# Sliding-window attention and a gMLP on one Trainium2 core: the same steps in a new hand-written order, with 75 passes on other engines and 37 products in another form

## The chip, the cores and the metric

One core of a Trainium2 chip (trn2). The metric is device time in microseconds of one execution. Each kernel is run several times; the median is given with the lowest and the highest run. A profiled execution gives a trace: every instruction's start and duration, by engine. The engines are TensorE (PE, with its weight loads as PEld), VectorE (DVE), ScalarE (ACT), GpSimd (POOL) and SyncE (SP), which here only issues DMAs.

## The reference

Inputs are float32: q, k, v of shape 8 x 8 x 576 x 64 (batch, heads, positions, head size), and the weights of the gMLP. The output is 8 x 576 x 512.

```
scores = q @ k^T / 8                          # per batch and head
scores = where(0 <= t - s < 64, scores, -1e9) # causal window of 64
attn   = softmax(scores);  x = attn @ v       # heads side by side: x is 8 x 576 x 512
h      = relu(x @ w_in);   u, v2 = h[..., :512], h[..., 512:]
v_n    = (v2 - mean(v2)) / sqrt(var(v2) + 1e-6)         # over the last axis
v_s    = w_spatial @ v_n + b_spatial          # mixes positions, per batch
out    = (u * v_s) @ w_out
```

## The kernel before, in words

**Work.** The eight batches go one after the other through attention (two groups g of four heads) and the gMLP, overlapped. Each batch's 576 positions are four tiles of 128 and a remainder of 64. The remainder's attention is done for both groups together (name ending `_r`), in batches 4 and 5, and 6 and 7, for two batches at once (PAIRS). Compute is in float16 with float32 sums in PSUM.

**Steps.** All work is cut into about 1100 named steps, each on one engine. A step's name has its batch, its group or tile:

- `ldq ldk ldv` are DMA loads issued by SP (lines 412, 433); `ldwin ldwsp ldwo ldb` load the weights and the bias; `st` are stores.
- `cq ck cv`, `cwin cwsp cwo cb` cast what was loaded to float16 (helper `cp`, lines 290 to 300; on GpSimd a q or k tile is three casts of 384 columns, line 295). `tq tk` are VectorE's 32x32 transposes of q and k (line 419). `sl su s4` copy v into a shifted layout (lines 449 to 459).
- `S` are the scores (TensorE, line 479), `E` the exponentials (ScalarE, 486), `M` the mask as a minimum (VectorE, 489), `Z` the row sums by a product with ones (TensorE, 502), `N` and `n` the logarithm and exp(-log) that invert them (ScalarE, 529, 531), `P` the product with v (514), `X` the scaling of it (VectorE, 522). The remainder's scores are on line 553, its `Z_r` on 582, `P_r` on 597.
- `V` and `U` are x @ w_in's two halves (TensorE, 614 or 617; the last tile of V together with the previous batch's last tile of the output, 702 and 705). `Vr` and `Ur` evict them with a ReLU (ScalarE, 669 and 763). `Vb Va` are VectorE's mean and variance (671, 673), `L1 L2` ScalarE's 1/sqrt (716, 718), `A` the normalisation (VectorE, 728).
- `G` is the product with the transposed w_spatial (five contraction tiles kk, the last with the bias row), `Ge` its eviction times u (VectorE, 797), `O` the product with w_out, `Oe` its copy out of PSUM (line 647), then the store.
- `W` transposes w_spatial on TensorE (378), `We` copies it out (384). `D` are warming steps: two matmuls of zeros into a bank that nobody reads (862); two of the 27 have nine short ones instead (line 149).

**Order.** Nothing schedules at run time. `ORDER` (line 18) lists every step with its engine and its buffers: `V0_2:PE:1` is batch 0, tile 2, on TensorE, in PSUM bank 1. Each engine runs its steps in the listed order and waits at semaphores for what the step's instructions read or overwrite. `DQ` is SP's queue of DMA issues. The pairs of numbers behind the steps' names in the code, such as `("ACT", 0.49)`, are the engines that a step may have and its planned cost; they are not used at run time.

**Forms.** `halves` (line 612) emits a gMLP product in one of two forms. With `PE` in the list each matmul has 128 weight columns (line 614). With `PH` each is two matmuls of 64 weight columns, into the lower and the upper half of the PSUM bank (line 617).

**Buffers.** Eight buffers for natural tiles (`nat`), four for v, nine for the transposed ones, four PSUM banks and two pairs of banks (the scores). A load is issued when the buffer's last reader is done.

## Time and profile before

| | us |
|---|---|
| runs: lowest, median, highest | 195.38, 195.44, 198.58 |
| profiled execution: from its first to its last instruction (the span) | 193.6 |
| what the median has beside that span | 1.84 |
| TensorE busy in the span | 184.9 |
| VectorE, ScalarE, GpSimd busy | 163.7, 157.1, 87.4 |
| first scores S0_0 start on TensorE | 9.26 |
| second group of batch 1, S1_1, starts | 29.85 |
| first G product starts | 38.69 |
| last product starts | 188.93 |

The page gives the span of the profiled execution and not its whole time; the runs above were timed without a profile. HBM was read for 32.79 MB and written for 9.44 MB, 218 GB/s over the span.

How to read the rows that follow: a row of a timeline is start, duration, engine, line, operation, out<-in, shape, count, and in brackets the idle time of the engine before it with what ended it. Alike instructions that follow each other are one row, and its duration goes from the first one's start to the last one's end. Matmuls are pipelined, so a row's duration has the last one's way through the array in it; the distance from one product's start to the next one's is what it costs. A row of a view by stage is from:to, length, then busy time and count of each engine. A group's row is line, engine, operation, out<-in, shape, count, busy us, mean ns of one, and idle us before it.

### The profile page before, as it was taken

Reading aid. Unit: us, or ns where it says so; the run is one execution under the profiler, and the core shown is the slowest. Engines: PE = TensorE matmul, PEld = TensorE weight load, DVE = VectorE, ACT = ScalarE, POOL = GpSimd, SP = SyncE. Lnnn points to the kernel's source line nnn. Section 1 sums busy time; section 2 is a strip of 40 time slices with the busy share of each in tenths; the row PEclk is TensorE's granted clock in tenths of the full one; section 3 lists DMA queues with packets and bytes.
Section 4 is the critical chain, followed back from the end, with each engine's and each line's share of the span. In section 5 each row is a group of like instructions: output and inputs, shape, how many; then the busy total and the mean of one; then the engine's idle time right before and its main releaser. Section 6 shows DMA issues by size and latency. Waiting matters only on the chain.

```text
span 193.6 us, 7606 instructions
## 1 busy us (share of the span) xinstructions
PE 184.9 (95%) x3218; PEld 107.0 (55%) x3218; DVE 163.7 (85%) x304; ACT 157.1 (81%) x282; POOL 87.4 (45%) x161
## 2 busy tenths in 40 slices
...
GB/s 177 373 316 290 391 355 333 168 275 373 242 205 332 261 335 179 149 38 289 367 230 184 310 310 282 196 177 218 306 125 266 22 3 0 224 30 0 135 166 191
DMA packets 50421, 42.73 MB, mean 221 GB/s; under 512 B 39377, under 2 KB 39761, under 8 KB 50386
## 3 DMA queue, kind: packets, MB, share of 16 engines
...
q8 instruction: 25, 0.41, 0.9%
...
HBM read 32.79 MB, written 9.44 MB: 218 GB/s over the span
## 4 chain that ended last, share of the span: by engine, by line
PE 70%; DVE 13%; ACT 9%; DMA 3%; issue 2%; SPq 1%
PE bank L617 50%; PE bank L614 4%; PE pair L479 4%; PE bank L514 3%; DMA nk<-in_k_dram 3%; PE bank L502 3%; ACT e L486 3%; DVE qT L419 2%; PE bank L702 2%; DVE e L489 2%; DVE kT L419 2%; DVE st L671 2%; DVE g L797 1%; DVE x L522 1%; ACT lz L529 1%
## 5 line engine op out<-in xcount | busy, mean ns | idle before, releaser
L617 PE MATMUL bank<-wspT,vn 128*64 128x512 f16 (+3 forms) x530 | 39.1, 296 | 0.0
L486 ACT ACTIVATE e<-pair 128x1024 f16<-128x1024 f32 x32 | 32.0, 1030 | 1.6 <-PE pair L479 1.4
L797 DVE TENSOR_TENSOR g<-bank,ru 128x512 f16<-128x512 f32 (+1 forms) x36 | 23.3, 654 | 9.4 <-PE bank L617 7.0
L647 ACT COPY ob<-bank 128x512 f32<-128x512 f32 (+1 forms) x38 | 21.9, 591 | 9.7 <-PE bank L617 8.4
L669 ACT ACTIVATE vs<-bank 128x512 f16<-128x512 f32 (+1 forms) x40 | 23.8, 602 | 7.1 <-PE bank L705 5.6
L617 PE MATMUL bank<-x,win 128*64 128x512 f16 (+2 forms) x304 | 29.1, 327 | 0.0
L617 PEld LDWEIGHTS <-vn 128*64 128x64 f16 (+1 forms) x530 | 20.8, 111 | 13.2 <-issue 0.2
L671 DVE BATCH_NORM_STATS2 st<-vs 128x6 f32<-128x512 f16 (+1 forms) x40 | 26.0, 670 | 2.3 <-ACT vs L669 2.2
L298 POOL COPY hs<-hv 64x512 f16<-64x512 f16 (+1 forms) x36 | 20.1, 585 | 16.3 <-ACT hv L292 8.4
L617 PE MATMUL bank<-win,x 128*64 128x512 f16 x216 | 27.0, 379 | 0.0
L617 PE MATMUL bank<-wout,g 128*64 128x512 f16 (+1 forms) x208 | 24.7, 371 | 0.0
L522 DVE TENSOR_TENSOR x<-bank,lz 128x512 f16<-128x512 f32 x32 | 21.2, 684 | 3.5 <-PE bank L514 2.2
L489 DVE TENSOR_TENSOR e<-e,mask 128x1024 f16<-128x1024 f16 x32 | 23.0, 725 | 0.5 <-ACT e L486 0.4
L763 ACT ACTIVATE ru<-bank 128x512 f32<-128x512 f32 (+1 forms) x38 | 21.6, 584 | 1.5 <-PE bank L617 0.8
L295 POOL CAST hk<-nk 128x384 f16<-128x384 f32 x36 | 19.4, 574 | 7.1 <-DMA nk<-in_k_dram 6.7
L529 ACT ACTIVATE lz<-bank 128x512 f32<-128x512 f32 x32 | 19.0, 599 | 1.9 <-PE bank L502 1.6
L298 POOL CAST hv<-nv 128x512 f16<-128x512 f32 x18 | 11.7, 661 | 18.8 <-DMA nv<-in_v_dram 18.7
L419 DVE STREAM_TRANSPOSE kT<-hk 128x576 f32<-128x576 f32 x16 | 19.9, 1241 | 0.2 <-ACT hk L292 0.2
L419 DVE STREAM_TRANSPOSE qT<-hq 128x576 f32<-128x576 f32 x16 | 19.8, 1237 | 0.2
L531 ACT ACTIVATE lz<-lz 128x512 f32<-128x512 f32 x32 | 19.6, 642 | 0.0
L295 POOL CAST hq<-nq 128x384 f16<-128x384 f32 x27 | 14.9, 588 | 10.3 <-DMA nq<-in_q_dram 7.8
L617 PEld LDWEIGHTS <-win 128*64 128x64 f16 x304 | 14.4, 110 | 9.2
...
## 6 DMA issues: line engine op xcount, KB each, us to landing
...
nv<-in_v_dram SPq DMA_DIRECT2D x64, 128.0 KB, 5.9
...
wi<-in_moe_w_in_dram SPq DMA_DIRECT2D x8, 256.0 KB, 5.8
...
wo<-in_moe_w_out_dram SPq DMA_DIRECT2D x4, 256.0 KB, 7.2
```

The lines of the kernel that those rows point to most:

```text
L295: nc.gpsimd.tensor_copy(o[:, n:n + 384], i[:, n:n + 384])
L298: nc.gpsimd.tensor_copy(o[:, lo:hi, :, :], i[:, lo:hi, :, :])
L419: d = add(f"t{name}{b}_{g}", ("DVE", 1.09), key, lambda e: nc.vector.transpose(qt.t[:, :].rearrange("p (i j) -> p j i", j=18), h.t[:, :].b ...
L486: ex = add(f"E{b}_{g}{u}", ("ACT", 0.91), key, lambda e, u=u: nc.scalar.activation(e2[u].t[:, :, :], sc[u].t[:, :, :], AF.Exp, bias=0.0, s ...
L489: mins.append(add(f"M{b}_{g}{u}", ("DVE", 0.65), key, lambda e, u=u: nc.vector.tensor_tensor(e2[u].t[:, :, :], e2[u].t[:, :, :], mask[:, : ...
L522: lambda e, u=u, ob=ob, lz=lz: nc.vector.tensor_tensor(x.t[:, u, :], ob.t[:, :], lz.t[:, :], ALU.mult),
L617: nc.tensor.matmul(o[c:c + 64, :], w[:, c:c + 64], x, start=start, stop=stop)
L647: lambda e: (nc.vector.tensor_copy if last else nc.scalar.copy)(view(), m.t[rows, 0:n]),
L669: rl = add(f"Vr{b}_{j}", ("ACT", 0.49), key, lambda e: nc.scalar.activation(vs.t[0:jn, :], m.t[0:jn, :], AF.Relu), deps=[pv], acq=[vs], us ...
L671: s1 = add(f"Vb{b}_{j}", ("DVE", 0.6), key + 0.02, lambda e: nc.vector.bn_stats(st6.t[0:jn, 0:6], vs.t[0:jn, :]), deps=[rl], acq=[st6], us ...
L763: lambda e, m=m, ru=ru, n=n: nc.scalar.activation(ru.t[:, 0:n], m.t[:, 0:n], AF.Relu), deps=[pu], acq=[ru], uses=[m])))
L797: nc.vector.tensor_tensor(g.t[:, 0:n], m.t[:, 0:n], ru.t[:, 0:n], ALU.mult)
```

## The change

ORDER is another list of the same steps without seven of the warming steps: 27 become 20, all of two matmuls of 512 columns. Every engine's sequence is new, SP's of the loads and stores too, and the buffers are dealt anew.

75 passes have another engine. From ScalarE to VectorE: seven `Oe`, seven `Ur`, five `Vr`, and `cwin110 s40_0 sl1_11 su1_00`. From ScalarE to GpSimd: 18 casts and copies, among them `ck3_1 cq7_0 cq7_1`, five `cv` and `cwo00`. From VectorE to GpSimd: ten, among them `cq1_1 cq6_0`. From VectorE to ScalarE: `ck0_0 cq0_0 cq0_1 We0 We4 sl0_10 Oe7_3 Oe7_4`. From GpSimd to ScalarE: `cb ck2_0 cv5_10 s46_0`, two `sl` and three `su`; to VectorE: `ck6_0 cwsp0`, three `sl` and two `su`. In sum ScalarE has 24 steps fewer, VectorE and GpSimd 12 more each.

37 gMLP products have the other form: 23 halved ones become full (V0_3, V1_1, V1_2, V2_0, V2_1, U0_2, U0_3, U1_1, U1_3, U1_4, U2_0, G1_4, G7_0 to G7_4, O6_2, O6_3, O7_0, O7_2, O7_3, O7_5) and 14 full ones halved (U1_0, U2_2, U2_4, U3_2, U3_3, U3_4, G2_0, G2_2, G2_3, G2_4, O1_1, O1_2, O1_3, O2_2).

The diff, with ORDER cut to the start (up to the first G products) and the close (from V7_4 on):

```diff
@@ ORDER @@
-D24:PE:0 ldb:DQ:0 D5:PE:1 D21:PE:2 ldk0_0:DQ:1 ck0_0:DVE:0 tk0_0:DVE:0 D18:PE:3 D2:PE:2 D14:PE:2
-D19:PE:3 D10:PE:0 ldq0_0:DQ:2 ldk0_1:DQ:3 ldv0_00:DQ:0 ldq0_1:DQ:4 ldv0_10:DQ:1 D3:PE:3 ldv0_11:DQ
-cv0_10:POOL:0 ldk1_0:DQ:5 ck0_1:ACT:1 ldv0_12:DQ ldv0_13:DQ ldv0_01:DQ cq0_0:DVE:2 ldq1_0:DQ:6
-tq0_0:DVE:1 ldv0_02:DQ D1:PE:2 S0_0:PE:0:1 tk0_1:DVE:2 D22:PE:0 E0_01:ACT:0 E0_00:ACT:1 cq0_1:DVE:3
-tq0_1:DVE:3 D15:PE:3 D6:PE:1 D0:PE:2 D26:PE:0 D23:PE:3 S0_r:PE:1:0 E0_r0:ACT:0 E0_r1:ACT cv0_11:POOL
-sl0_10:DVE:0 M0_00:DVE ldv0_03:DQ su0_10:DVE M0_01:DVE ck1_0:DVE:0 M0_r:DVE D8:PE:1 Z0_00:PE:2
-ldv0_04:DQ ldwin110:DQ:7 ldv0_14:DQ ldwin111:DQ ldwin100:DQ:1 S0_1:PE:1:0 N0_00:ACT:0 E0_11:ACT:2
-D16:PE:0 D7:PE:3 E0_10:ACT:3 M0_11:DVE Z0_01:PE:1 Z0_r:PE:2 D4:PE:0 Z0_11:PE:3 N0_r:ACT:1
-N0_01:ACT:2 cv0_00:ACT:1 N0_11:ACT:3 ldwin101:DQ su0_11:DVE M0_10:DVE D12:PE:0 Z0_10:PE:2 D20:PE:1
-sl0_11:POOL tk1_0:DVE:4 sl0_00:ACT:1 N0_10:ACT:4 n0_11:ACT n0_10:ACT cq1_0:POOL:2 tq1_0:DVE:5
-ldq1_1:DQ:2 ldk1_1:DQ:3 P0_10:PE:0 P0_11:PE:3 cwin110:ACT n0_01:ACT D11:PE:1 cv0_01:POOL
-ldwin000:DQ:4 ldwin010:DQ:5 ldwin001:DQ ldwin011:DQ ldwsp1:DQ:6 X0_10:DVE:0 su0_00:DVE X0_11:DVE
-n0_00:ACT sl0_01:POOL cb:POOL su0_01:POOL S1_0:PE:0:1 D25:PE:2 D13:PE:1 P0_00:PE:0 X0_00:DVE:1
-E1_01:ACT:3 s40_1:ACT P0_01:PE:2 D9:PE:3 cwin111:POOL cwin100:POOL cwin101:POOL ck1_1:POOL:1
-s40_0:ACT E1_00:ACT:2 cwin010:POOL X0_01:DVE cwin001:POOL cwin011:POOL V0_2:PE:1 M1_01:DVE
-Vr0_2:ACT:0 n0_r:ACT P0_r:PE:3 Z1_01:PE:0 V0_0:PE:2 ldwsp3:DQ:0 M1_00:DVE N1_01:ACT:5 Vr0_0:ACT:1
-cq1_1:DVE:3 Z1_00:PE:1 V0_3:PH:0 V0_1:PE:2 N1_00:ACT:4 cwin000:ACT Vr0_3:ACT:2 Vr0_1:ACT:3
-ldwsp0:DQ:7 ldwsp4:DQ:1 ldwsp2:DQ:2 cwsp1:POOL:6 ldv1_00:DQ:2 ldq2_0:DQ:3 X0_r:DVE:0 tq1_1:DVE:7
-Vb0_2:DVE:0 V0_4:PE:3 tk1_1:DVE:8 S1_1:PE:1:0 cwsp3:POOL:0 cwsp0:POOL:1 Vb0_0:DVE:1 Vb0_3:DVE:2
-Vr0_4:ACT:4 Va0_3:DVE Vb0_4:DVE:3 Va0_4:DVE Va0_0:DVE Va0_2:DVE Vb0_1:DVE:4 Va0_1:DVE U0_2:PH:1
-U0_3:PH:0 ldk2_0:DQ:4 U0_4:PE:2 ldv1_01:DQ ldv1_02:DQ ldv1_03:DQ E1_11:ACT:1 E1_10:ACT:0 cwsp2:POOL
-cq2_0:POOL:0 M1_10:DVE ldv1_10:DQ:3 Ur0_2:ACT:0 L10:ACT:0 ldv1_11:DQ ldv1_12:DQ ldv1_13:DQ L20:ACT
-ldv1_14:DQ ldq2_1:DQ:5 ldv1_04:DQ ldk2_1:DQ:6 ldwo00:DQ:0 ldwo01:DQ Ur0_4:ACT:1 S1_r:PE:0:1
-Z1_10:PE:3 U0_0:PE:1 ldwo10:DQ:7 ldwo11:DQ U0_1:PE:2 E1_r0:ACT:0 Ur0_3:ACT:2 E1_r1:ACT Ur0_0:ACT:3
-N1_10:ACT:3 A0_0:DVE:0 A0_3:DVE:1 cwsp4:DVE Ur0_1:ACT:4 W1:PE:0 W3:PE:1 W2:PE:3 W0:PE:2 A0_1:DVE:2
-A0_4:DVE M1_11:DVE We1:DVE M1_r:DVE n1_00:ACT We2:ACT We3:ACT A0_2:DVE:3 We0:DVE W4:PE:0 ldq3_0:DQ:1
-ldk3_0:DQ:2 ldv2_00:DQ:1 ck2_0:POOL:2 We4:DVE D17:PE:3 Z1_11:PE:1 Z1_r:PE:2 G0_0:PH:3 G0_1:PH:0
...
-Ge6_4:DVE:0 Ge6_1:DVE:1 st5_4:DQ st5_1:DQ st5_0:DQ G6_0:PH:3 Ge6_0:DVE:2 Vb7_2:DVE:5 V7_4:PE:0
-U7_1:PH:2 G6_3:PH:3 Vr7_4:ACT:2 Oe6_4:ACT:0 Ur7_1:ACT:5 Ur7_3:ACT:0 Vb7_1:DVE:2 Va7_0:DVE
-Vb7_4:DVE:4 Va7_4:DVE Ge6_3:DVE:3 Va7_1:DVE Va7_2:DVE L17:ACT:1 L27:ACT A7_4:DVE A7_1:DVE:4
-A7_0:DVE:5 A7_2:DVE:6 U7_2:PH:0 O6_1:PH:2 O6_2:PH:1 O6_0:PH:3 Ur7_2:ACT:3 Oe6_0:ACT:0 Oe6_1:ACT
-O6_3:PH:0 Oe6_2:ACT:1 Oe6_3:ACT A7_3:DVE:7 G7_0:PH:3 st6_0:DQ st6_4:DQ st6_1:DQ G7_1:PH:2 G7_2:PH:1
-G7_3:PH:0 Ge7_0:DVE:5 Ge7_1:DVE:6 Ge7_2:DVE:7 G7_4:PH:3 Ge7_3:DVE:8 O7_0:PH:2 Oe7_0:ACT:0 st7_0:DQ
-O7_2:PH:1 Oe7_2:ACT:1 Ge7_4:DVE:9 O7_1:PH:0 st7_2:DQ O7_3:PH:3 O7_4:PE:2 Oe7_1:ACT O7_5:PH:1
-Oe7_3:DVE st7_1:DQ st7_3:DQ Oe7_5:ACT Oe7_4:DVE:0 st7_41:ACT st7_40:DQ st7_5:ACT
+D0:PE:0 D1:PE:1 D2:PE:2 D3:PE:3 D4:PE:0 D5:PE:1 D6:PE:2 D7:PE:3 ldv0_00:DQ:0 ldk0_0:DQ:0 ldq0_0:DQ:1
+ck0_0:ACT:0 ldk0_1:DQ:2 cq0_0:ACT:1 tk0_0:DVE:0 tq0_0:DVE:1 ldq0_1:DQ:3 D8:PE:0 D9:PE:1 D10:PE:2
+D11:PE:3 S0_0:PE:0:1 D12:PE:0 ck0_1:ACT:2 D13:PE:1 cq0_1:ACT:3 ldb:DQ:4 tk0_1:DVE:2 tq0_1:DVE:3
+ldk1_0:DQ:5 ldv0_01:DQ ldq1_0:DQ:6 ldv0_10:DQ:1 E0_00:ACT:0 ldv0_11:DQ E0_01:ACT:1 ldv0_02:DQ
+D14:PE:2 D15:PE:3 D16:PE:0 S0_r:PE:0:1 M0_00:DVE ldv0_14:DQ ldv0_03:DQ ldv0_13:DQ Z0_00:PE:1
+M0_01:DVE ldv0_12:DQ cv0_00:POOL:0 sl0_00:POOL:0 cq1_0:POOL:0 cb:ACT E0_r0:ACT:0 cv0_10:POOL:1
+cv0_01:POOL su0_01:POOL su0_00:POOL E0_r1:ACT ldwin110:DQ:7 ldv0_04:DQ N0_00:ACT:0 ldwin100:DQ:0
+Z0_01:PE:2 S0_1:PE:0:1 ldwin111:DQ cv0_11:POOL ck1_0:DVE:1 M0_r:DVE ldwin101:DQ E0_10:ACT:2
+ldq1_1:DQ:1 ldk1_1:DQ:2 tk1_0:DVE:4 N0_01:ACT:1 ldwin010:DQ:3 ldwin000:DQ:4 cwin111:POOL
+cwin100:POOL cwin101:POOL ldwin011:DQ D17:PE:3 Z0_r:PE:0 ldwin001:DQ ldwsp3:DQ:5 cq1_1:POOL:2
+N0_r:ACT:2 sl0_10:ACT:1 ck1_1:POOL:3 ldwsp0:DQ:6 ldwsp4:DQ:0 cwin010:POOL ldwsp2:DQ:1 M0_10:DVE
+tq1_0:DVE:5 E0_11:ACT:3 cwin001:POOL cwin011:POOL ldwsp1:DQ:2 sl0_01:DVE su0_10:DVE M0_11:DVE
+ldq2_0:DQ:3 cwsp3:POOL:6 D18:PE:3 ldv1_00:DQ:2 cwsp2:POOL n0_00:ACT n0_r:ACT ldv1_01:DQ cwsp1:POOL:7
+su0_11:DVE cwin110:DVE sl0_11:DVE s40_0:DVE ldk2_0:DQ:7 Z0_10:PE:3 D19:PE:1 S1_0:PE:0:1 N0_10:ACT:3
+n0_01:ACT s40_1:ACT P0_00:PE:1 Z0_11:PE:2 N0_11:ACT:4 n0_11:ACT n0_10:ACT cwsp4:POOL X0_00:DVE:0
+P0_10:PE:0 P0_r:PE:3 cq2_0:POOL:1 ldv1_03:DQ X0_r:DVE:0 ldv1_02:DQ cv1_00:POOL:2 P0_01:PE:2
+E1_01:ACT:0 P0_11:PE:1 sl1_00:POOL:2 X0_01:DVE X0_10:DVE:1 ldv1_10:DQ:3 V0_4:PE:3 X0_11:DVE
+cv1_01:POOL E1_00:ACT:2 Vr0_4:ACT:0 M1_01:DVE M1_00:DVE V0_0:PE:2 ldv1_11:DQ su1_01:POOL ldv1_13:DQ
+ldv1_12:DQ tq1_1:DVE:8 ldv1_14:DQ V0_2:PE:0 tk1_1:DVE:0 V0_1:PE:1 Vr0_2:ACT:1 cwin000:ACT
+Vr0_1:ACT:2 Vr0_0:ACT:3 V0_3:PE:3 Vb0_2:DVE:0 Vb0_4:DVE:1 ldv2_00:DQ:1 ldk2_1:DQ:4 Z1_01:PE:0
+cv1_10:POOL:3 Va0_2:DVE sl1_10:POOL:3 cv1_11:POOL N1_01:ACT:5 Vr0_3:ACT:4 S1_1:PE:1:0 E1_11:ACT:1
+Vb0_3:DVE:2 Vb0_1:DVE:3 su1_10:POOL U0_2:PE:1 ldq2_1:DQ:5 M1_11:DVE Va0_3:DVE Vb0_0:DVE:4
+ldwo10:DQ:1 Va0_1:DVE ldv1_04:DQ E1_10:ACT:3 Ur0_2:ACT:0 U0_4:PE:2 U0_0:PE:0 Va0_0:DVE Ur0_0:ACT:1
+ldwo00:DQ:2 Va0_4:DVE S1_r:PE:0:1 Z1_11:PE:3 s41_1:POOL U0_3:PE:1 ldwo11:DQ ck2_1:POOL:0 cwsp0:DVE:1
+ldwo01:DQ ldk3_0:DQ:6 U0_1:PE:0 Ur0_4:DVE:2 W2:PE:2 cq2_1:POOL:2 s41_0:POOL cwo10:POOL E1_r0:ACT:0
+L10:ACT:0 E1_r1:ACT L20:ACT Ur0_3:ACT:3 W1:PE:1 A0_1:DVE:0 cwo11:POOL N1_11:ACT:0 A0_2:DVE:1
+M1_r:DVE M1_10:DVE Ur0_1:ACT:4 W4:PE:3 cwo01:POOL We2:ACT A0_4:DVE ldv2_02:DQ ldv2_01:DQ ldq3_0:DQ:0
+ldv3_00:DQ:0 ldv2_03:DQ W0:PE:0 ldv2_10:DQ:3 ldv3_02:DQ ldv2_14:DQ We1:DVE cwo00:POOL We4:ACT
+W3:PE:2 We0:ACT Z1_00:PE:3 Z1_10:PE:1 We3:ACT N1_10:ACT:2 A0_0:DVE:2 ck2_0:ACT:3 A0_3:DVE:3
+tq2_0:DVE:2 G0_3:PH:0 Z1_r:PE:2 Ge0_3:DVE:0 N1_00:ACT:1 G0_0:PH:1 N1_r:ACT:3 n1_10:ACT tk2_0:DVE:3
...
+Ur7_4:DVE:3 G6_2:PH:3 Ge6_3:DVE:1 G6_4:PH:1 Ge6_2:DVE:0 U7_0:PH:0 Ge6_4:DVE:2 G6_0:PH:2 V7_4:PE:3
+Ge6_0:DVE:3 U7_2:PH:1 Va7_1:DVE Vb7_0:DVE:2 Oe6_4:ACT:0 Vr7_4:DVE:0 O6_0:PH:2 Ur7_2:ACT:4 Va7_0:DVE
+Vb7_4:DVE:3 O6_1:PH:3 Oe6_0:ACT:1 Va7_4:DVE Ur7_0:DVE:5 L17:ACT:1 O6_2:PE:1 L27:ACT Oe6_1:ACT
+A7_1:DVE:4 A7_4:DVE O6_3:PE:2 A7_0:DVE:5 Oe6_2:ACT:0 A7_3:DVE:6 A7_2:DVE:7 G7_1:PE:0 Oe6_3:ACT
+st6_1:DQ G7_0:PE:3 st6_0:DQ st6_4:DQ G7_2:PE:1 Ge7_0:DVE:8 Ge7_1:DVE:6 G7_3:PE:2 Ge7_2:DVE:5
+Ge7_3:DVE:7 O7_0:PE:3 O7_2:PE:0 Oe7_0:ACT:0 st7_0:DQ O7_5:PE:1 Oe7_2:ACT:1 G7_4:PE:2 st7_2:DQ
+Oe7_5:DVE O7_3:PE:3 st7_5:ACT Ge7_4:DVE:9 O7_4:PE:0 Oe7_3:ACT O7_1:PH:1 st7_3:DQ Oe7_4:ACT:0
+st7_40:DQ st7_41:ACT Oe7_1:DVE st7_1:DQ
-NWARM, NFILL, FILL = 27, 2, 9
+NWARM = len([w for w in ORDER.split() if w[0] == "D"])
@@ -298,6 +298,12 @@
             ENG[e].tensor_copy(o, i)
+
+    def relu(e, o, i):
+        if e == "ACT":
+            nc.scalar.activation(o, i, AF.Relu)
+        else:
+            nc.vector.tensor_scalar_max(o, i, 0.0)
@@ -643,8 +649,8 @@
         def view():
-        cpy = add(f"Oe{b}_{j}", ("DVE", 0.4) if last else ("ACT", 0.49), key,
-                  lambda e: (nc.vector.tensor_copy if last else nc.scalar.copy)(view(), m.t[rows, 0:n]),
+        cpy = add(f"Oe{b}_{j}", cost(n, p=False, d1=True), key,
+                  lambda e: cp(e, view(), m.t[rows, 0:n]),
@@ -666,8 +672,8 @@
     def stat_steps(b, j, m, vs, pv, key, VS, ST):
-        rl = add(f"Vr{b}_{j}", ("ACT", 0.49), key, lambda e: nc.scalar.activation(
-            vs.t[0:jn, :], m.t[0:jn, :], AF.Relu), deps=[pv], acq=[vs], uses=[m])
+        rl = add(f"Vr{b}_{j}", [("ACT", 0.49), ("DVE", 0.61)], key, lambda e: relu(
+            e, vs.t[0:jn, :], m.t[0:jn, :]), deps=[pv], acq=[vs], uses=[m])
@@ -759,9 +765,9 @@
-            RU.append((ru, add(f"Ur{tag}", ("ACT", 0.06 + 0.00083 * n), key + 0.2 + 0.03 * i,
-                               lambda e, m=m, ru=ru, n=n: nc.scalar.activation(
-                                   ru.t[:, 0:n], m.t[:, 0:n], AF.Relu), deps=[pu], acq=[ru], uses=[m])))
+            RU.append((ru, add(f"Ur{tag}", cost(n, p=False, d1=True), key + 0.2 + 0.03 * i,
+                               lambda e, m=m, ru=ru, n=n: relu(
+                                   e, ru.t[:, 0:n], m.t[:, 0:n]), deps=[pu], acq=[ru], uses=[m])))
@@ -857,9 +863,8 @@
         def emit_D(e, m=m, i=i):
-            for c in range(2 if i < NWARM - NFILL else FILL):
-                n = 512 if i < NWARM - NFILL else 128
-                nc.tensor.matmul(m.t[:, 0:n], scratch[:, 0:128], scratch[:, 0:n], start=True, stop=True)
+            for c in range(2):
+                nc.tensor.matmul(m.t[:, :], scratch[:, 0:128], scratch[:, :], start=True, stop=True)
         add(f"D{i}", ("PE", 0.43), -2.0, emit_D, acq=[m], mode="f")
```

179 lines of the change are left out of this document (88 added, 91 removed).

## The prediction

> **What bounds the kernel now.** I read the page first (busy shares, then the chain that ended last), then the busy time by stage, then the timelines of TensorE and VectorE up to the first G product, then those of the last 20 us.
>
> ```profile
> span 193.6 us, 7606 instructions
> PE 184.9 (95%) x3218; PEld 107.0 (55%) x3218; DVE 163.7 (85%) x304; ACT 157.1 (81%) x282; POOL 87.4 (45%) x161
> PE 70%; DVE 13%; ACT 9%; DMA 3%; issue 2%; SPq 1%
> ```
>
> TensorE is the engine of the chain (70%). The next view splits its time at S0_0 (first scores, 9.25), S1_1 (29.85), the first G product (38.69) and the last product; the one behind it is the same for the warming matmuls (L862) alone.
>
> ```profile
> 9.25:29.85 20.60, 18.98 (x335) 8.85 (x336) 19.29 (x27) 17.73 (x32) 13.17 (x20) 1.00 1.10 333
> 29.85:38.69 8.84, 8.60 (x147) 5.06 (x149) 8.51 (x22) 8.12 (x17) 6.29 (x9) 1.00 0.92 252
> 38.69:189.40 150.71, 150.33 (x2723) 90.53 (x2719) 129.66 (x241) 128.53 (x232) 65.61 (x121) 1.00 0.69 201
> ```
>
> ```profile
> 9.25:29.85 20.60, 8.61 (x46) 3.00 (x46) 1.00 1.10 333
> ```
>
> The columns are PE, PEld, DVE, ACT and POOL busy, the granted clock, the DMA share and GB/s. From 38.69 on TensorE is idle for 0.38 us of 150.71: nothing but less TensorE work, or an earlier start of this stage, can gain there. Before 29.85, 8.6 of its 18.98 busy us are warming, that is, waiting in disguise, while VectorE is busy for 19.29 of 20.60. So the start is paced by VectorE and its suppliers, the rest by TensorE, and a warming step taken out gains nothing by itself.
>
> **The amount of TensorE work.** The new order holds the same real products. Ahead of the first G product (G0_0 before, G0_3 after) the two orders have the same products done but for two small ones, Z1_r before and Z1_00 in both. So the question is when the first G product starts, what TensorE loses after it, and how the kernel closes.
>
> Change of form, 37 products: a full product is 4 matmuls, a halved one 8.
>
> ```profile
> 76.96 2.75 PE L614 MATMUL bank<-wout,g 128*128 128x512 f16 x12
> 79.55 0.63 PE L614 MATMUL bank<-x,win 128*128 128x64 f16 x16
> 177.04 3.62 PE L617 MATMUL bank<-wout,g 128*64 128x512 f16 x32
> 180.50 5.14 PE L617 MATMUL bank<-wspT,vn 128*64 128x512 f16 x80
> 73.81 0.38 PE L502 MATMUL bank<-e,ones 128*64 128x512 f16 x2
> 74.02 1.03 PE L617 MATMUL bank<-x,win 128*64 128x512 f16 x8
> 81.33 0.39 PE L502 MATMUL bank<-e,ones 128*64 128x512 f16 x2
> 81.65 4.04 PE L614 MATMUL bank<-wspT,vn 128*128 128x512 f16 x35
> ```
>
> Three full products go from 76.96 to 79.55, 0.863 us each; four halved ones from 177.04 to 180.50, 0.865. The form itself costs nothing. A switch between 64-column and 128-column weights does: Z then a halved product is 0.21 (73.81 to 74.02), Z then a full one 0.32 (81.33 to 81.65), so 0.1 a switch. Counted in the two orders, there are 16 such switches from the first G product on in both (28 against 23 from S0_0 on, the five being in the start, where waiting covers them). Term: 0.
>
> **The start.** VectorE's and GpSimd's rows of the stage that decides:
>
> ```profile
> 7.16 0.75 DVE L300 CAST hq<-nq 128x1152 f16<-128x1152 f32 x1
> 25.60 1.06 DVE L300 CAST hq<-nq 128x1152 f16<-128x1152 f32 x1
> 28.56 1.23 DVE L419 STREAM_TRANSPOSE kT<-hk 128x576 f32<-128x576 f32 x1
> 37.53 0.82 DVE L300 COPY wspT<-bank 128x576 f16<-128x576 f16 x2
> 17.10 1.90 POOL L295 CAST hq<-nq 128x384 f16<-128x384 f32 x3 [1.02 <-DVE e L489]
> 25.20 2.28 POOL L295 CAST hk<-nk 128x384 f16<-128x384 f32 x3 [1.79 <-DMA nk<-in_k_dram]
> 27.43 1.72 POOL L300 CAST win<-wi 128x512 f16<-128x512 f32 x3
> 17.70 0.33 SPq L412 DMA_DIRECT2D nq<-in_q_dram  x1
> DMA to landing us min/median/max: 5.4/5.9/6.4
> ```
>
> Before, VectorE itself casts q of batch 1, heads 4 to 7 (25.60, 1.06 us), then transposes it, and starts k's transpose tk1_1 at 28.56, though k was cast by 27.48. After, cq1_1 is GpSimd's, ahead of ck1_1. The same loads stand ahead of q1_1 and k1_1 in both orders, and DMA is full (share 1.10), so I leave their landings: q1_1 at 17.70 + 5.4 = 23.1, k1_1 at 25.2. GpSimd: 23.1 + 1.90 = 25.0, then k from 25.2 in 1.72 (three casts undisturbed, the 27.43 row, an upper neighbour in size) to 2.28 (as now): 26.9 to 27.5, I take 27.2. VectorE sheds ck0_0, cq0_0, cq0_1, cq1_1 (0.75 to 1.06 each) and takes cwin110 and three small copies, so it should be free by then: tk1_1 starts at 27.2, 1.4 us earlier.
>
> The first load is now v, one issue and 128 KB ahead of k, and the first casts are ScalarE's (row below: 1.16 instead of 0.75). Both make S0_0 later, by an estimated 0.3 us, but ScalarE takes all four casts and VectorE is free between transposes, so the masks of heads 0 to 3 come no later than now.
>
> ```profile
> L292 ACT CAST hq<-nq 128x1152 f16<-128x1152 f32 x3 | 3.5, 1156 | 0.0
> 29.85 0.67 PE L479 MATMUL pair<-qT,kT 32*128 32x128 f16 x56 [0.42 <-DVE kT L419]
> 35.48 2.39 PE L378 MATMUL bank<-id,wn 128*128 128x128 f16 x25
> 37.80 0.61 PE L862 MATMUL bank<-scratch 128*128 128x512 f16 x2
> ```
>
> From tk1_1 to the first G, VectorE does the same in both orders but for Vb0_2 (0.6) and Ur0_4 (0.41) added and We0 and We4 (0.82 the pair) gone to ScalarE: 28.56 to 38.35 is 9.79, after 9.9. It ends with A0_0 and A0_3: 27.2 + 9.9 = 37.1. G0_3 needs A0_0 first, a third of a us earlier, and A0_3 only with its fourth matmul pair, so it can start at 36.8. TensorE's own chain from S1_1 (27.2 + 1.23 = 28.5) is the 8.84 of now less the warming step at 37.80 (0.54) and a wait of 0.3 at S1_r: 28.5 + 8.1 = 36.6, in time. The W transposes (35.48 now) come some 1.8 us earlier, and the casts of W_spatial that they need, four of them on GpSimd, are taken as in time. **First G product: 36.8 in place of 38.69, -1.9 us.** Bounds: -2.5 (q1_1 and k1_1 landing 0.6 sooner) to -0.8 (the later first casts carry through, 0.3, and both GpSimd casts run as slowly as the slowest now).
>
> **From the first G to the last batch.** 19 of the 75 moved passes are evictions from ScalarE to VectorE, 17 of 512 columns and 2 of 256. VectorE's 512-column copy out of PSUM has no row; bounds are the 256-column copy and the two-input product, and I take the latter, of the same size.
>
> ```profile
> L647 DVE COPY ob<-bank 128x256 f32<-128x256 f32 x1 | 0.4, 426 | 0.1
> L797 DVE TENSOR_TENSOR g<-bank,ru 128x512 f16<-128x512 f32 x32 | 21.8, 684 | 9.3 <-PE bank L617 7.0 <-ACT ru L763 1.4 <-ACT lz L531 0.4
> 60.00:80.00 20.00, 20.00 (x345) 12.20 (x332) 19.50 (x35) 19.56 (x36) 15.12 (x28) 1.00 0.91 253
> 170.00:180.00 10.00, 10.00 (x122) 5.58 (x118) 7.53 (x18) 3.41 (x8) 0.00 (x0) 1.00 0.02 7
> ```
>
> 17 x 0.684 + 2 x 0.42 = 12.5 us more for VectorE (7.3 to 12.5). All but two stand in batches 4 to 7, beside a TensorE that is full while VectorE, in 170 to 180, is busy for 7.5 of 10 us: hidden. Without that cover, each is 0.68 us between a product and the next one on its bank. 28 passes, copies and casts of loads and weights, go to GpSimd and 16 leave it: net three loads of 1.7 us and nine shorter passes, an estimated 10 us on its 87.4, off the chain. In 60 to 80 VectorE is busy for 19.5 of 20: there a lead of TensorE can be spent by waiting for it. Counted in the order, VectorE's work ahead of S3_1 falls from 60 to 54 us while TensorE's falls from 47 to 44, so most of the lead should hold. I take **+0.3** (bounds -0.4, the idle time of now, and +1.9, all of the lead).
>
> One rule speaks against this. VectorE's cast of 1152 took 0.75 us while GpSimd rested (7.16) and 1.06 while it cast (25.60). The Trainium skill, page "SBUF — State Buffer", section "Who interferes with whom", says that VectorE in a two-port mode, or with two inputs in SBUF, and GpSimd block each other for a whole instruction; the rows agree. By that rule ck1_1 would take its 2.28 again, and the start would gain 1.6 in place of 1.9.
>
> **The close.**
>
> ```profile
> 185.11 0.69 DVE L797 TENSOR_TENSOR g<-bank,ru 128x512 f16<-128x512 f32 x1 [0.39 <-PE bank L617]
> 188.93 0.61 PE L617 MATMUL bank<-wout,g 128*64 128x256 f16 x8
> 189.57 0.37 ACT L835 COPY ob<-bank 128x256 f32<-128x256 f32 x1 [0.72 <-PE bank L617]
> 190.31 0.54 ACTq L838 DMA_DIRECT2D out_dram<-ob  x1
> out_dram<-ob SPq DMA_DIRECT2D x3, 256.0 KB, 2.1
> out_dram<-ob ACTq DMA_DIRECT2D x1, 128.0 KB, 2.4
> ```
>
> G7_3's last matmul is issued by 184.83 (20 pairs of halves at 0.216 from 180.50), Ge7_3 ends at 185.80, 0.97 later. Now G7_4 (0.63) stands between G7_3 and O7_0; after, O7_0 follows at once, and its fourth matmul, 0.65 in, waits 0.3. G7_4 comes later, with one half-size product (0.44, the 188.93 row to 189.37) ahead of O7_4, which waits about 0.2 for Ge7_4 (256 wide, 0.4). **+0.5**. After the last product, now 189.37 by issue: copy to 189.94, store issued at 190.31 behind another, landing 2.4 later, 192.7. After, the last is the full O7_1: copied by VectorE (0.2 + 0.68), issued at once on SP, 2.1 to land: 3.05 against 3.35. **-0.25**, rounded.
>
> **Sum.** -1.9 + 0.3 + 0.5 - 0.25 = -1.35. Against the profiled execution: span 193.6 - 1.35 = 192.25. The median of the runs is 195.44, 1.84 above that span; what lies around it is taken as unchanged: 194.1 us.
>
> **Rivals.**
> - *The lead is spent* (20%): GpSimd's extra 10 us slow VectorE's masks and casts (1.06 against 0.75) while VectorE is already at 19.5 of 20, and TensorE waits for 1.9 us more between 40 and 130. Against it: VectorE has less listed ahead of each S. Time: 195.44 + 0.5 - 0.25 = 195.7.
> - *TensorE runs cold* (10%), the case on the slower side. At the start it needs 6.87 us for 20 matmuls:
>
> ```profile
> 1.27 6.87 PE L862 MATMUL bank<-scratch 128*128 128x512 f16 x20 [1.27 <-DVE scratch L237]
> ```
>
>   At the 0.216 of the rows of 76.96 (12 in 2.59), 20 would take 4.3, so a cold stretch costs 2.5 us. After S0_0 the order keeps 8 warming steps of 17, and only D18 and D19 between the masks of heads 0 to 3 and V0_4. If it goes cold there and the V0 and U0 products pay 2.5, the first G is at 39.3: +0.6 + 0.3 + 0.5 - 0.25 = 196.6. It decides once the loss passes 1.4. Against it: between the listed products I count no pause over some 1.3 us. The Trainium skill, "TensorE: Matmul & The Clock Gate", section "What's actually happening", gives half rate after an idle window of about 3.4 us, which by that count does not come.
> - *All of it holds* (15%): the first G at -2.5, the 0.4 idle gone, no wait at O7_0: 195.44 - 2.5 - 0.4 - 0.25 = 192.3.
> - The forecast 50%, 5% for what I don't see.
>
> **How the numbers follow.** The range 191.9 to 196.8 holds the rivals' times with the bounds of the start. 2% is 3.9 us, about what a measurement of this kernel can tell from no change (its runs go from 195.38 to 198.58). Faster by more than that needs more than the best case gives: 6%. Slower by more needs two cold stretches or a mishap: 5%.
>
> **What would show it.** Right: first G product near 36.8, S1_1 near 28.5, no idle time over 1 us from there to the last product, a wait of 0.3 at O7_0, the last store on SP. Wrong: S1_1 at 29.8 or later (the start did not gain), TensorE idle for over 1 us between 40 and 130 (lead spent), matmul groups at 0.43 us after 15 us (cold).

## The result: 202.09 us where 194.1 was forecast, and the profile after

After takes 202.09 us (median of four runs), before 195.81 beside it on the same chip: a ratio of 1.029, 95% interval 1.023 to 1.035. All ratios here leave out runs in a slower state that some executions show (one of the four, 205.14). The forecast was 194.1, its range 191.9 to 196.8. The profiled execution of after took 201.66 us, its span is 199.9, 6.3 more than before's.

The page of after, the lines that answer to the three shown first:

```profile
span 199.9 us, 7491 instructions
PE 185.1 (93%) x3149; PEld 107.1 (54%) x3149; DVE 174.6 (87%) x316; ACT 146.6 (73%) x258; POOL 101.4 (51%) x180
PE 43%; DVE 29%; DMA 10%; ACT 6%; SPq 5%; issue 5%; POOL 0%; DVEq 0%; POOLq 0%; ACTq 0%
```

TensorE's share of the chain fell from 70 to 43%; VectorE, DMA and SP's queue took it. TensorE's busy time is as before, with seven warming steps less in it and some products at a slower clock (see below), so most of the 6.3 us is waiting. The busy time by stage, split at the same four points (S0_0, S1_1, first G product, end of the last product):

```profile
9.27:30.10 20.83, 16.07 (x298) 8.01 (x298) 19.76 (x27) 17.05 (x28) 14.64 (x23) 0.92 1.01 303
30.10:38.78 8.68, 8.42 (x137) 4.76 (x135) 7.84 (x20) 8.53 (x18) 5.82 (x9) 1.00 1.01 274
38.78:195.70 156.92, 152.72 (x2694) 91.42 (x2692) 141.59 (x256) 117.00 (x210) 78.65 (x138) 1.00 0.67 196
```

Two things are to be seen. The first G product starts at 38.78, against 38.69 before and 36.8 forecast: the start gained nothing. And from there to the end of the last product it is 156.92 us against 150.71, with 4.20 us of visible idle time against 0.38: 6.2 us lost where the prediction took +0.3 and +0.5. (A stall costs some 0.2 us more than its idle time: below, 2.0 lost beside 1.84 idle, and 1.2 beside 0.17 and 0.63, since the last matmul's way through the array still counts as busy. So distances between the starts of products are used below.)

**Where TensorE waited.** TensorE's timeline of after, the rows with the long waits, and the close:

```profile
60.94 0.39 PE L623 MATMUL bank<-wspT,vn 128*64 128x512 f16 x2
...
62.53 0.84 PE L623 MATMUL bank<-wspT,vn 128*64 128x512 f16 x6 [0.63 <-DVE vn L734]
63.21 0.28 PE L588 MATMUL bank<-er,ones 128*64 128x128 f16 x4
...
82.80 1.34 PE L623 MATMUL bank<-wspT,vn 128*64 128x512 f16 x10 [0.16 <-ACT ob L292]
84.90 0.41 PE L508 MATMUL bank<-e,ones 128*64 128x512 f16 x2 [0.77 <-ACT ob L292]
...
131.17 1.89 PE L623 MATMUL bank<-win,x 128*64 128x512 f16 x16
134.91 2.35 PE L623 MATMUL bank<-wspT,vn 128*64 128x512 f16 x20 [1.84 <-DVE vn L734]
...
190.59 2.64 PE L620 MATMUL bank<-wout,g 128*128 128x512 f16 x12
193.06 0.76 PE L620 MATMUL bank<-wspT,vn 128*128 128x64 f16 x20
193.66 0.60 PE L620 MATMUL bank<-wout,g 128*128 128x256 f16 x4
194.34 0.63 PE L852 MATMUL bank<-wout,g 128*64 128x256 f16 x8
```

- G1_0 goes from 60.94 to 63.21, 2.27 us for ten matmuls that take 1.08 elsewhere: **1.2 lost**, waiting for batch 1's normalisations (A1) on VectorE.
- G2_0 goes from 82.80 to 84.90, 2.10 in place of 1.08, and starts 0.3 late: **1.3 lost**, waiting for banks that ScalarE's copies of batch 1's output (Oe1) had not yet emptied.
- V5_1 and V5_2 start at 131.17 and need 1.73 (16 x 0.108), but G4_3 follows at 134.91: **2.0 lost**, waiting for A4 on VectorE.
- The close: O7_0, O7_2 and O7_5 take 2.47 (190.59 to 193.06) in place of 2.16, and O7_4 comes 0.68 behind O7_3 in place of 0.44: **0.55 lost**, as the prediction had it (0.3 and 0.2).

These are 5.1 of the 6.2; the rest are waits of 0.1 to 0.35, such as one of 0.35 ahead of Z5_10.

**What was late behind the three waits.** First VectorE's timeline of after about 60 us, with the five A1 (L734), then GpSimd's:

```profile
59.12 1.37 DVE L734 TENSOR_SCALAR vn<-vs,mv,ln 128x512 f16<-128x512 f16 x2
60.41 0.41 DVE L580 TENSOR_TENSOR er<-er,mask 128x512 f16<-128x512 f16 x1
60.74 1.74 DVE L734 TENSOR_SCALAR vn<-vs,mv,ln 128x512 f16<-128x512 f16 x3
```

```profile
58.12 2.22 POOL L298 COPY hs<-hv 64x512 f16<-64x512 f16 x4
60.40 0.89 POOL L298 CAST hv<-nv 128x512 f16<-128x512 f32 x1
```

The five A1 take 3.1 us, 0.62 each, while GpSimd copies and casts beside them; the group's mean before was 0.43. The three GpSimd steps (sl2_00, su2_00, cv2_10) are among the moved passes. For the second wait, SP's queue in after, the issues of st0_0 and st0_1, and ScalarE's row of Oe1_2:

```profile
73.91 1.90 SPq L668 DMA_DIRECT2D out_dram<-ob  x1
...
77.67 0.44 SPq L668 DMA_DIRECT2D out_dram<-ob  x1
```

```profile
84.27 0.58 ACT L292 COPY ob<-bank 128x512 f32<-128x512 f32 x1 [1.52 <-DMA out_dram<-ob]
```

Oe1_2 waits 1.52 us for its output buffer. The store that frees it, st0_1, was issued at 77.67, though its data had been ready since 60.1: in SP's queue it stood behind thirteen loads (and two stores), issued one by one from 61.2 on. For the third wait, GpSimd's and VectorE's timelines of after:

```profile
127.15 2.24 POOL L295 CAST hk<-nk 128x384 f16<-128x384 f32 x3 [5.99 <-DVE st L677]
...
131.54 1.17 POOL L298 CAST hv<-nv 128x512 f16<-128x512 f32 x2 [1.59 <-DMA nv<-in_v_dram]
```

```profile
132.19 0.73 DVE L300 COPY hs<-hv 64x768 f16<-64x768 f16 x1 [1.03 <-POOL hv L298]
132.94 2.52 DVE L734 TENSOR_SCALAR vn<-vs,mv,ln 128x512 f16<-128x512 f16 x4
```

sl7_10, a copy of batch 7 that TensorE first needs at 162 us (P7_10), was moved to VectorE and stands ahead of four of the A4. It waits for cv7_10, which was moved to GpSimd and waits there for a load; so VectorE stands still for 1.03 us, and the four A4 then take 0.63 each.

**The start.** The timelines of VectorE, GpSimd and TensorE in after:

```profile
25.51 1.59 DVE L495 TENSOR_TENSOR e<-e,mask 128x1024 f16<-128x1024 f16 x2
...
28.12 1.23 DVE L425 STREAM_TRANSPOSE kT<-hk 128x576 f32<-128x576 f32 x1
...
31.33 1.29 DVE L677 BATCH_NORM_STATS2 st<-vs 128x6 f32<-128x512 f16 x2 [0.83 <-ACT vs L304]
```

```profile
24.11 1.41 POOL L295 CAST hq<-nq 128x384 f16<-128x384 f32 x3 [0.89 <-DMA nq<-in_q_dram]
25.95 1.96 POOL L295 CAST hk<-nk 128x384 f16<-128x384 f32 x3 [0.44 <-DMA nk<-in_k_dram]
```

```profile
23.92 1.89 PE L708 MATMUL bank<-win,x 128*64 128x512 f16 x4
25.75 4.08 PE L620 MATMUL bank<-win,x 128*128 128x512 f16 x16
29.76 0.41 PE L508 MATMUL bank<-e,ones 128*64 128x512 f16 x2
```

q1_1 and k1_1 landed 0.8 to 1.0 later than taken (casts at 24.11 and 25.95 for 23.1 and 25.2), and tk1_1 starts at 28.12 for 27.2. Beside that, the 20 matmuls of V0 take 5.84 us (23.92 to 29.76), at 0.216 they would take 4.32. The busy time by stage shows why, in the column behind the five engines, the granted clock:

```profile
19.40:20.91 1.51, 0.44 (x24) 0.35 (x15) 1.42 (x4) 1.49 (x4) 0.94 (x2) 1.00 0.81 215
20.91:22.60 1.69, 0.52 (x8) 0.33 (x7) 1.63 (x4) 1.23 (x4) 1.04 (x2) 1.00 0.96 319
...
23.92:25.75 1.83, 1.83 (x14) 0.52 (x10) 1.83 (x4) 1.04 (x2) 1.41 (x3) 0.50 0.94 338
```

TensorE is busy for 0.96 of 3.20 us, waiting for masks and a copy; in the next 1.3 us its mean clock is 0.77, and then 0.50. VectorE in its turn waits 0.83 us at 31.33 for an eviction of V0.

### The profile page after: what moved, and what is told of

It reads as the page before. It is cut to its first block, busy times and chain, and to the rows that moved or that the text cites. A ratio compares the mean times of both kernels' runs of the same rounds, so it can differ in the third digit from the quotient of the medians.

```text
span 199.9 us, 7491 instructions
## 1 busy us (share of the span) xinstructions
PE 185.1 (93%) x3149; PEld 107.1 (54%) x3149; DVE 174.6 (87%) x316; ACT 146.6 (73%) x258; POOL 101.4 (51%) x180
## 4 chain that ended last, share of the span: by engine, by line
PE 43%; DVE 29%; DMA 10%; ACT 6%; SPq 5%; issue 5%; POOL 0%; DVEq 0%; POOLq 0%; ACTq 0%
PE bank L623 28%; PE bank L620 7%; DVE e L495 5%; DVE vn L734 4%; DVE st L677 4%; DMA nq<-in_q_dram 4%; DMA out_dram<-ob 3%; DMA nv<-in_v_dram 3%; DVE x L528 3%; SPq L439 2%; DVE g L803 2%; DVE qT L425 2%; DVE kT L425 2%; DVE hs L300 2%; PE bank L708 2%
## 5 line engine op out<-in xcount | busy, mean ns | idle before, releaser
L292 ACT COPY ob<-bank 128x512 f32<-128x512 f32 (+2 forms) x33 | 19.0, 581 | 16.9 <-PE bank L620 5.8
L304 ACT ACTIVATE vs<-bank 128x512 f16<-128x512 f32 (+1 forms) x35 | 20.6, 598 | 9.7 <-PE bank L623 6.0
L295 POOL CAST hq<-nq 128x384 f16<-128x384 f32 x39 | 23.5, 636 | 5.7 <-DMA nq<-in_q_dram 5.1
L295 POOL CAST hk<-nk 128x384 f16<-128x384 f32 x33 | 18.7, 603 | 13.2 <-DMA nk<-in_k_dram 7.0
L495 DVE TENSOR_TENSOR e<-e,mask 128x1024 f16<-128x1024 f16 x32 | 25.1, 791 | 0.2
L623 PE MATMUL bank<-wout,g 128*64 128x512 f16 x192 | 24.5, 380 | 0.0
L623 PE MATMUL bank<-win,x 128*64 128x512 f16 x176 | 21.7, 380 | 0.0
L304 ACT ACTIVATE ru<-bank 128x512 f32<-128x512 f32 (+1 forms) x31 | 17.9, 581 | 5.1 <-PE bank L623 4.4
L298 POOL COPY hs<-hv 64x512 f16<-64x512 f16 (+1 forms) x34 | 19.3, 599 | 0.8
L734 DVE TENSOR_SCALAR vn<-vs,mv,ln 128x512 f16<-128x512 f16 (+1 forms) x40 | 17.9, 494 | 0.1
```

The source lines that it names most:

```text
L295: nc.gpsimd.tensor_copy(o[:, n:n + 384], i[:, n:n + 384])
L298: nc.gpsimd.tensor_copy(o[:, lo:hi, :, :], i[:, lo:hi, :, :])
L304: nc.scalar.activation(o, i, AF.Relu)
L495: mins.append(add(f"M{b}_{g}{u}", ("DVE", 0.65), key, lambda e, u=u: nc.vector.tensor_tensor(e2[u].t[:, :, :], e2[u].t[:, :, :], mask[:, : ...
L623: nc.tensor.matmul(o[c:c + 64, :], w[:, c:c + 64], x, start=start, stop=stop)
L734: ENG[e].tensor_scalar(o[0:jn, :], VS[j].t[0:jn, :], mv_t[b % NSB][0:jn, j, 0:1], ln.t[0:jn, 5 + j:6 + j], ALU.subtract, ALU.mult)
```

## The experiments

Theory A: the loss sits in a few passes that stand late in their queues, at the places above. Theory B: it is the load, VectorE's and GpSimd's added work and their slowing each other. All runs are medians beside before on the same chip (195.7 to 196.1); a ratio is to before.

**Order or engines alone.** The 75 passes back on the engines of before, in the order of after; and the other way round.

```diff
 order of after
-cv7_10:POOL:1
+cv7_10:ACT:1
-sl7_10:DVE:2
+sl7_10:POOL:2
...
```

> The order of after, with the 75 moved passes on the engines they had before (forms and warming as after). Theory A (a few passes stand late in their queues: the waits at 61, 82 and 132 us and a cold stretch at 24): the wait at 132 goes, because sl7_10 leaves VectorE and cv7_10 leaves GpSimd, the other three stay: 199.5 to 200.5. Theory B (the load: VectorE's 10.9 us and GpSimd's 14 us more, and their slowing each other): most of the loss goes with the moves: 195.5 to 197.

Measured: 229.85 us, ratio 1.174 (1.169 to 1.179).

```diff
 order of before
-cv7_10:ACT:3
+cv7_10:POOL:3
...
```

> The order, forms and warming of before, with the 75 passes on the engines of after. Theory A: each pass stands where its inputs are early, so 195.5 to 197. Theory B: VectorE is as loaded as in after, TensorE waits for it: 199 or more.

Measured: 214.5 us, ratio 1.097 (1.092 to 1.103). Both theories missed by far. Either half alone is much worse than the whole change: in the order of after on the old engines TensorE once waits 9.3 us for a mask (Z, at 26.35), and on the new engines in the old order GpSimd's casts of v wait for their loads for 28 us in sum, at places of the list that were made for ScalarE and VectorE. A step's place in the list is right for one engine's queue only. So the change can't be split into a share of the order and a share of the engines, and smaller parts were tried.

**The forms alone.**

```diff
 order of before
-G7_0:PH:3
+G7_0:PE:3
-U1_0:PE:0
+U1_0:PH:0
...
```

> Before, with only the 37 products in the form of after. Prediction's term 0: 195.2 to 196.0. Rival (a full product is slower than a halved one, or loses its hidden weight loads): 23 full against 14 halved, at 0.1 us each at most 2.3 us more: 197 or more.

Measured: 198.65 us, ratio 1.014 (1.011 to 1.017): 2.9 us, the rival. It isn't that a full product is slower. Counted in the lists with the scores, S, whose rows show 128 columns too, both before and after switch between 64 and 128 weight columns 30 times from the first G on; before with the forms of after switches 55 times. The 25 more, at the 0.1 worked out in the prediction, are 2.5. The profile of this run has a wait beside them:

```profile
125.51 0.38 PE L708 MATMUL bank<-win,x 128*64 128x512 f16 x1 [0.92 <-ACT ru L304]
```

From the first G to the last product's start it takes 3.37 longer than before (39.16 to 192.77, before 38.69 to 188.93). Of that 1.1 is this wait, and the other 2.3 fit the 25 switches at 0.09 each. So the forms belong to the order, and by the count of switches they cost nothing in the change as a whole, as forecast.

**The cold stretch.** Five warming steps where TensorE paused.

```diff
-S1_0:PE:0:1 P0_00:PE:1 Z0_11:PE:2 P0_10:PE:0
+S1_0:PE:0:1 P0_00:PE:1 D20:PE:0 D21:PE:0 Z0_11:PE:2 D22:PE:3 D23:PE:3 D24:PE:3 P0_10:PE:0
```

> After with five warming steps more between S1_0 and P0_10. Cold theory: V0_4's four pairs go in 1.05 us in place of 1.85 and the four V0 products behind it in 3.5 in place of 4.0; the first G comes 1 to 1.5 us earlier (37.4) and the time is 200.6 to 201.1. Rival (VectorE sets the start in any case): the V0 products are quicker but S1_1 and the first G move by at most 0.5 and the time stays at 201.6 to 202.1.

Measured: 202.36 us, ratio 1.029 (1.020 to 1.037), no gain. The clock held; stage, then GpSimd's and TensorE's rows of this run:

```profile
23.90:28.60 4.70, 4.70 (x27) 1.76 (x20) 3.39 (x6) 2.17 (x4) 2.36 (x5) 1.00 1.02 392
```

```profile
26.24 1.87 POOL L295 CAST hq<-nq 128x384 f16<-128x384 f32 x3 [2.53 <-DVE e L495]
```

```profile
30.82 0.67 PE L485 MATMUL pair<-qT,kT 32*128 32x128 f16 x56 [1.81 <-DVE kT L425]
```

V0 takes 4.70 in place of 5.84, but now S1_1 waits 1.81 us for k's transpose, since q1_1 was cast only at 26.24 in this run, and the first G stands at 38.80. (The bracket of the cast names a mask; what came last was the load of q1_1, landed at 26.12, 2.1 later than in after.) The cold stretch was real, and the time is as the rival has it, but this run doesn't decide between the two, since its loads came later. Behind them VectorE needed 9.0 us from tk1_1 to the last of A0 (29.50 to 38.48) without a wait for V0's evictions, where it needs 10.9 in after. In after, k's transpose ended at 29.35 and S1_1 started at 30.10, so up to 0.75 us came through to S1_1. What the clock alone costs stays open.

**The two late passes, one at a time and together.**

```diff
-sl7_10:DVE:2 Ur5_2:ACT:4 A4_3:DVE:1 A4_1:DVE:2 V5_2:PH:2 A4_0:DVE:3 Vr5_1:ACT:7 A4_4:DVE
+Ur5_2:ACT:4 A4_3:DVE:1 A4_1:DVE:2 V5_2:PH:2 A4_0:DVE:3 Vr5_1:ACT:7 A4_4:DVE sl7_10:DVE:2
```

> After with one step moved: the copy sl7_10 stands behind the five A4 on VectorE and not ahead of four of them. Theory A (VectorE's queue stands behind a copy whose cast on GpSimd waits for a load): the wait of G4_3 at 132 us, 2.0, shrinks to 0.3 or less, the time falls by 1.5 to 2.0, to 200.1 to 200.6. Theory B (VectorE is too loaded, another wait takes its place): the wait returns elsewhere within 20 us and the time falls by less than 0.5.

```diff
-st0_0:DQ ldv4_12:DQ ldk5_0:DQ:0 st0_1:DQ
+st0_0:DQ st0_1:DQ ldv4_12:DQ ldk5_0:DQ:0
```

> After with one store, st0_1, moved up in SP's queue, ahead of the loads ldv4_12 and ldk5_0. Theory A: Oe1_2 on ScalarE finds its output buffer free at 82.8 and not at 84.3, Z3_01 loses its wait of 1.0, the time falls by 0.8 to 1.3. Theory B (DMA is full, the store pushes the loads back and a cast waits in its place): no change, within 0.4.

> After with both moves, of sl7_10 and st0_1. Theory A: the gains add up, 2.3 to 3.3 less, 198.8 to 199.8. Theory B: less than 1 in all.

Measured: 201.31 (ratio 1.025, 1.020 to 1.029), 201.36 (1.025, 1.020 to 1.030) and, with both, 201.2 (1.024, 1.020 to 1.029): 0.7 to 0.9 less than after each, and no more together. These intervals overlap with that of after, so the gains themselves are not established by the times. Each wait did go where it was aimed at. In the run with the late copy G4_3 starts 0.3 late in place of 2.0; what comes back shows 5 us later:

```profile
132.20 2.35 PE L623 MATMUL bank<-wspT,vn 128*64 128x512 f16 x20
...
137.28 0.41 PE L508 MATMUL bank<-e,ones 128*64 128x512 f16 x2 [0.75 <-DVE g L806]
```

In the run with the early store, Oe1_2 follows Oe1_1 at once and Z3_01 comes 1.08 behind G2_0:

```profile
82.49 1.05 ACT L292 COPY ob<-bank 128x512 f32<-128x512 f32 x2
```

So A has the places and the causes right, and B the sum: of the 3.3 us that both moves free (2.0 and 1.3) the times give back 0.9. For the copy, half of the 2.0 is lost again at 137.28, as shown. For the store the profile doesn't show it: in its profiled run, the quickest of six (199.70), the way from the first G to the last product's start is 2.0 shorter than in after, while the median is 0.7 less. The waits also differ from run to run; in the run with five warming steps the one at 84.90 is absent, with nothing changed there. So one profile's wait isn't a fixed price.

**GpSimd's load, in before.**

```diff
+    for i in range(29):
+        add(f"K{i}", ("POOL", 0.6), -2.0, lambda e: cp(e, scratch[:, 0:512], scratch[:, 0:512]))
```

> Before with 29 idle copies of 128x512 on GpSimd (a zeroed buffer onto itself, no part of the computation), put where GpSimd had nothing to do between 54 and 132 us: its busy time rises by some 17 us, from 87 to 105, a little over what the change adds. Contention theory (GpSimd slows VectorE's masks and normalisations, and TensorE then waits): masks at 790 ns and A at 490 in place of 725 and 422, and 1.5 us or more on the time: 197.2 or more. Rival (what is slowed lies beside TensorE's work): 195.4 to 196.2.

Measured: 198.56 us, ratio 1.012 (1.008 to 1.015). GpSimd's busy time rose by 24 us (111.5), 0.83 a copy, more than I had reckoned. The groups of before, then of this run:

```profile
L489 DVE TENSOR_TENSOR e<-e,mask 128x1024 f16<-128x1024 f16 x32 | 23.0, 725 | 0.5 <-ACT e L486 0.4
L728 DVE TENSOR_SCALAR vn<-vs,mv,ln 128x512 f16<-128x512 f16 x32 | 12.1, 422 | 2.2 <-ACT ln L718 1.9
```

```profile
L492 DVE TENSOR_TENSOR e<-e,mask 128x1024 f16<-128x1024 f16 x32 | 26.3, 826 | 0.3 <-ACT e L489 0.2
L731 DVE TENSOR_SCALAR vn<-vs,mv,ln 128x512 f16<-128x512 f16 x32 | 15.2, 519 | 1.8 <-ACT ln L721 1.8
```

Masks rise from 725 to 826 ns, A of 128 partitions from 422 to 519, and from the first G to the last product's start it takes 152.6 us (39.77 to 192.35) in place of 150.2 (38.69 to 188.93). Its first G was 1.1 later in this profile, with nothing changed ahead of 54 us. The only thing added is work on GpSimd that nobody waits for: contention costs TensorE some 2.3 us here. (Once, at 118.60, VectorE waits 1.06 us for a GpSimd cast that stands behind four of the copies; TensorE has no wait from 112 to 126.) In after, with 14 us more on GpSimd, the same groups are:

```profile
L495 DVE TENSOR_TENSOR e<-e,mask 128x1024 f16<-128x1024 f16 x32 | 25.1, 791 | 0.2
L734 DVE TENSOR_SCALAR vn<-vs,mv,ln 128x512 f16<-128x512 f16 x32 | 14.6, 491 | 0.0
```

**The evictions.** 15 of the 19, those of batches 4 to 7, to VectorE in before, and back to ScalarE in after.

```diff
 order of before
-Vr6_1:ACT:0
+Vr6_1:DVE:0
...
```

> Before with 15 of the 19 evictions (those of batches 4 to 7, without the last two of the close) on VectorE in place of ScalarE, at their place in the order of before. The prediction's term (hidden): 195.4 to 196.2. Rival (VectorE's 10 us more delay what TensorE waits for): 197 or more.

```diff
 order of after
-Vr5_3:DVE:5
+Vr5_3:ACT:5
...
```

> After with the same 15 evictions on ScalarE again. If VectorE's load in the second half costs the time: 1.5 us or more less than after, 200.5 or less. If the evictions lie beside TensorE's work: 201.5 to 202.5.

Measured: 202.06 us (1.030, 1.026 to 1.034) and 202.63 us (1.031, 1.026 to 1.036). In the order of before the evictions are not hidden at all, 6 us, 0.4 each. TensorE's rows of the first run:

```profile
170.16 1.92 PE L623 MATMUL bank<-win,x 128*64 128x512 f16 x16 [1.35 <-DVE ob L300]
...
176.09 1.27 PE L623 MATMUL bank<-wspT,vn 128*64 128x512 f16 x10 [1.41 <-DVE ru L306]
```

A product waits for its bank, which VectorE empties only when it comes to that place of its list; that VectorE has idle time in sum in 170 to 180 doesn't help. In the order of after, which was made with them, giving them back gains nothing, though VectorE's busy time falls by 8.8 us. That doesn't show that VectorE's load costs nothing there, since places made for VectorE need not suit ScalarE, as the first two runs showed. But none of TensorE's waits in after ends with one of these evictions.

**Lighter masks.** The eight large masks of batches 1 and 2 on an eighth of their columns, in after and in before; both kernels leave the rest of these scores unmasked.

```diff
-                e2[u].t[:, :, :], e2[u].t[:, :, :],
+                e2[u].t[:, :, 0:512 // (8 if b in (1, 2) else 1)],
+                e2[u].t[:, :, 0:512 // (8 if b in (1, 2) else 1)],
```

> After with the eight large masks of batches 1 and 2 applied to an eighth of their columns only (the rest of these scores stays unmasked): VectorE has 8 times 0.7, 5.6 us less to do between 25 and 62 us. If VectorE paces TensorE there: the first G comes about 1.5 us earlier, G1_0's wait for A1 (1.2) goes, and the time is 2 to 3.5 less than after: 198.5 to 200. If loads and GpSimd's queue pace it: less than 1, 201 to 202.

> The same shortening in before, as the control. From the first G on TensorE has no idle time to give back, so only the start can gain: if VectorE paces the start, the first G is 1 to 1.5 us earlier and the time is 194.2 to 194.8; if TensorE's products and the landings pace it, within 0.4 of before, 195.3 to 196.0.

Measured: 200.89 us (ratio 1.026, 1.021 to 1.031) and 195.46 us (0.996, 0.993 to 0.998). The relief was smaller than meant: two of the eight rows in after,

```profile
32.37 0.57 DVE L495 TENSOR_TENSOR e<-e,mask 128x128 f16<-128x128 f16 x1
...
49.88 0.19 DVE L495 TENSOR_TENSOR e<-e,mask 128x128 f16<-128x128 f16 x1
```

0.19 us alone, up to 0.57 while GpSimd casts: VectorE's busy time fell by 2.5 us and not by 5.6. After gains 1.2 us by the medians but only 0.003 in the ratio, and the intervals overlap; before gains 0.6 (its first G at 38.06). In the profile of after 1.1 lies behind the first G: 0.4 at G1_0 (1.85 in place of 2.27), but 0.8 ahead of G4_3, in batch 4, whose masks weren't touched. No row shows how the masks could have caused that part. G1_0 still waits 0.54 us for A1, whose five passes take 2.7 us beside the same GpSimd steps. So VectorE paces TensorE at G1_0, in part; ScalarE's L21 ahead of A1 and GpSimd beside it hold the rest.

**The predicted start, in before.** cq1_1 on GpSimd ahead of ck1_1; in the first run also V0_4 behind S1_1, in the third also cwsp4 on GpSimd and no D17.

```diff
-ck1_1:POOL:1
+cq1_1:POOL:3 ck1_1:POOL:1
...
-cq1_1:DVE:3
...
-V0_4:PE:3 tk1_1:DVE:8 S1_1:PE:1:0
+tk1_1:DVE:8 S1_1:PE:1:0 V0_4:PE:3
```

> Before with the one move on which the predicted start rests: cq1_1 on GpSimd ahead of ck1_1 (and S1_1 ahead of V0_4 on TensorE, which would else stand in its way). The prediction's reading (VectorE paces the start): tk1_1 at 27.2 to 27.5 in place of 28.56, the first G 0.9 to 1.4 earlier, 194.4 to 195.0. Rival (the landings of q1_1 and k1_1 pace it): tk1_1 moves by 0.5 at most, the first G by 0.3 at most, 195.3 to 196.0.

> Before with cq1_1 alone on GpSimd ahead of ck1_1, TensorE's order as it was. If VectorE's 1.06 us paced the start: S1_1 follows V0_4 at once at 29.4, and VectorE's later passes bring the first G 0.5 to 1.0 earlier: 194.8 to 195.3. If TensorE's V0 products and the landings pace it: first G within 0.3, 195.5 to 196.0.

> Before with cq1_1 and cwsp4 on GpSimd in place of VectorE and without the warming step D17 ahead of the first G. If VectorE's passes pace the first G: it comes 0.4 to 0.8 earlier than with cq1_1 alone, 194.8 to 195.3. If it is paced elsewhere: as with cq1_1 alone, 195.4 to 195.9.

Measured: 197.29 us (1.006, 1.004 to 1.009), 195.67 us (0.997, 0.995 to 0.9996) and 195.70 us (0.997, 0.995 to 1.0001). In the first, VectorE waits 1.08 us at 32.00 for V0_4's eviction: TensorE's order there wasn't free either. The second is 0.3% under before, 0.4 us. From S1_0 to the first G it takes 17.6 us in place of 18.2 (21.09 to 38.71; before 20.49 to 38.69), but two runs above whose start is as before, those with the GpSimd copies and with the evictions, have 18.5 and 17.8. So the move gains some tenths, where the forecast had 1.9 for the first G. The third adds nothing (18.3 in its profile). In the second run the limit is TensorE; its stage from V0_2 to the first G:

```profile
24.02:38.71 14.69, 14.34 (x185) 7.26 (x186) 13.76 (x28) 13.85 (x27) 11.99 (x19) 1.00 1.00 299
```

TensorE is busy for 14.34 of 14.69 us there, 0.61 of it one warming step.

## Why the prediction was wrong, step by step

The sum was -1.35 on the span, and +6.3 came: 7.65 apart, 2.0 in the start, 5.4 in the middle, 0.25 in the closing store.

- **First G product at 36.8: failed**, 38.78. The step that failed is "the start is paced by VectorE and its suppliers", with the 8.6 us of warming as TensorE's reserve. The reserve lies ahead of V0. The stage from V0's start to the first G in before:

```profile
23.42:38.69 15.27, 14.40 (x183) 7.14 (x185) 14.51 (x30) 14.02 (x28) 10.86 (x16) 1.00 0.99 290
```

  TensorE is busy for 14.40 us there, as full as VectorE with 14.51. Its idle time, 0.87, and the one warming step (the row of 37.80, 0.54) come to 1.4, so a gain of 1.9 was more than there was to give. The prediction's chain for TensorE began at S1_1 and had nothing for V0, whose 20 matmuls stand ahead of it. With the one move on which the step rests, 0.4 came by the times. In after even this went: the landings, which I left as they were, came up to 1.0 later, VectorE needed 10.9 us from tk1_1 to the last of A0 in place of 9.9 (28.12 to 39.06, with the 0.83 of waiting at 31.33), and V0 ran cold.
- **Change of form, 0: right** for the change as a whole, by the count of switches; alone in the old order it is 2.9, by 25 switches and a wait. The 16 switches that the prediction counted in both orders don't come out of the lists: from the first G on it is 12 before and 8 after without the scores, and 30 in both with them.
- **The middle, +0.3 with a bound of +1.9: failed**, 5.7 (6.2 less the close). The step that failed is that VectorE's and GpSimd's added work would stay off TensorE's path. In part it is the rival "the lead is spent" (GpSimd slows VectorE's masks and A, TensorE waits between 40 and 135): beside GpSimd five A1 take 0.62 each in place of 0.43 and four A4 0.63 in place of 0.42, an estimated 1.8 of the 4.5 lost at the three waits. The rest is passes that stand late in a queue. The bound was wrong too: a lead limits what can be given back only if the waits come once. Here there was no lead, and each place where an input comes late costs in full, 1.2, 1.3 and 2.0. GpSimd's busy time rose by 14.0 us where I had estimated 10. I had counted the work listed ahead of each product, by engine; that says nothing of a pass that stands still in its queue (sl7_10, st0_1), and the durations in the count were those beside before's GpSimd.
- **The evictions, hidden: no wait of TensorE's in after ends with one, but for another reason** than the one given. VectorE's idle share hides nothing by itself (6 us in the old order); that the new list has each at the place where its bank is due is my reading of it.
- **The close, +0.5: right**, 0.31 and 0.24. **The closing store, -0.25: missed.** From the last issue to the end of the span it takes 4.24 us in both (189.36 to 193.6; 195.66 to 199.9). The store itself was nearly as forecast: by the traces it landed 3.12 us after the last issue (at 198.78) in place of 3.32 (192.68). The 0.2 went again between the landing and the end of the span, 1.16 us in place of 0.97, why is open.
- **TensorE runs cold**: given 10%, and it came, with 1.5 us for V0 in place of 2.5. "No pause over some 1.3 us" was right (1.07 and 1.17), and the clock fell all the same. What it cost is open: up to 0.75 at S1_1 and the 0.83 for which VectorE waited, and the run with five warming steps doesn't tell, because its loads came later.

What stays open: no run gave back more than 1.2 of after's 6.3. That a late copy and a late store make the second and the third wait, and that work on GpSimd costs TensorE time by itself, is shown by runs of their own. That contention makes the first wait is argued from the durations of A1, and the account of the start rests on single profiles whose first G scatters by up to 1.1. What the remaining small waits would cost with all of them mended at once was not tried.
